# Fixed turns for PSUM places in an attention and expert kernel, and P V's bank emptied one operation earlier

## The chip, the cores and the metric

The kernel runs on one core of a Trainium2 chip. Its time is the device time of one execution in microseconds (us). An execution is profiled once for the trace; three plain runs give the median.

## The reference

Attention over 8 batches and 8 heads: queries are averaged in twos (1152 to 576 rows), keys and values have 1152 rows of 64. Its result feeds a mixture of 8 experts that sends each of 4608 rows to one expert.

```python
q_pool = q.reshape(B, H, S // factor, factor, D).mean(axis=3)
scores = scale * np.matmul(q_pool, k.transpose(0, 1, 3, 2))
scores = scores - np.max(scores, axis=-1, keepdims=True)
attn = np.exp(scores)
attn = attn / (np.sum(attn, axis=-1, keepdims=True) + 1e-09)
...
logits = x @ w_gate
e_idx = np.argmax(logits, axis=1)
...
    h = np.maximum(x[mask] @ w1[e], 0.0)
    ye = h @ w2[e]
    out[mask] = gate_w[mask, None] * eom[mask, e, None] * ye
```

## The kernel before, in words

Two stages follow each other: the attention with the router (`attention`, the first 1090 us), and the experts (`Moe.run`). The change is in the first alone.

The attention goes over 32 **pairs** of heads. A pair takes 18 **steps**: a step makes one **chunk** of 128 keys of one head (9 chunks a head). Four streams are interleaved step by step, and the instructions of TensorE, VectorE, ScalarE and GpSimd stand in exactly the order in which the Python code emits them (`manual_schedule`):

- **Scores** (`scores`, L269 to L296): four matmuls (L279, L281) into a PSUM place of two banks; ScalarE takes two exponentials of it. In most chunks they go to a float32 and a float16 tile (L293, L294), and GpSimd subtracts one from the other (L295). In chunks 1, 3, 7, 9, 13, 15 of a pair (and in all odd chunks of the last pair) the second exponential is written back into PSUM (L285, L286), and VectorE subtracts (`lo`, L289) in the next step; only then is the place free. There are two places.
- **Maxima** (`mgen`, L210 to L243): for a later pair the row maxima of the scores, matmuls L232 into a bank and a VectorE reduction L233. A step has one or two of them in turn, two in odd steps. Behind each, `pop()` emits one waiting small operation.
- **P V** (`av`, L298 to L328): per chunk 15 matmuls (L308 to L310) into the single bank `av`, in bursts of 1 to 3 chunks at the end of even steps. A head's P V ends in step 4 or 14 of a pair, and the next head's starts two steps later, in step 6 or 16. Between them three VectorE operations empty the bank: e0 (L317), e1 (reciprocal, L320), e2 (the division into `xb`, L323). They are put at the front of the list `fill`.
- **The router** (`logits`, `router`): transposes L370, logits L385, then some 20 tiny VectorE operations on a batch every fourth pair. It keeps a PSUM place over several steps, twice: `tl`, then `rk`, whose last reader is the sum `cum` (L473).

`fill` is the list of small operations; `pop` takes from its front. It is called at the start of each step, behind each maximum, and with everything at the start of a head's P V. So before the change e0 comes at the start of step 15, e1 behind its first maximum, e2 behind its second.

PSUM has 8 banks: two places of two banks for scores (pool `ps_s`), one bank for P V, three for maxima and all small matmuls (pool `ps_m`, tag `mp`). The pools have several buffers under one tag, and the building layer chooses the place when it lays out the program, so a place need not follow in turn. In the built program the 18 chunks of pair 10 use the score banks 2 0 2 2 0 2 0 2 0 2 0 2 0 2 0 0 2 0: chunks 3 and 15 take the place that the chunk before them has just used. Banks of `mp` are taken in turn, 903 of 1106 times the one used three allocations before; 27 times it is the one used last.

The experts' first weight split (ScalarE cast L733, VectorE subtraction L734) is not under the fixed order, so the layer places it among the attention's last steps.

Of the kernel before, what the change touches and what calls it, by code (L numbers as in the profile page):

```python
# [8 lines left out]
F32 = mybir.dt.float32  # L9
# [8 lines left out]
PSUM = bass.MemoryType.PSUM  # L18
# [41 lines left out]
def attention(tc, qT, kT, vL, wg, keep, xrows, idscr, cum, pairs, setup, scat, init):  # L60
    nc = tc.nc
    nb = len(pairs) // 4
    with ExitStack() as ctx:
        def pool(name, bufs=1, **kw):
            return ctx.enter_context(tc.tile_pool(name=name, bufs=bufs, **kw))
# [6 lines left out]
        ep = pool("a_e")  # L72
        lp = pool("a_l")
        p3 = pool("a_p3")
        ps_s = pool("ps_s", 2, space=PSUM)
        ps_a = pool("ps_a", 1, space=PSUM)
        ps_m = pool("ps_m", 3, space=PSUM)

        ident = keep['ident']
        onesf = keep['onesf']  # L80
# [22 lines left out]
        def prep(n, table):  # L103
# [67 lines left out]
                nc.scalar.activation(out=j, in_=vp[:, NC * h:NC * h + NC], func=AF.Abs, scale=2.0 ** -17, accum_out=am[:, h:h + 1])  # L171

            def gmax():
                g = ps_m.tile([128, 512], F32, name="tp", tag="mp")[:, 0:2]
                nc.tensor.matmul(g, lhsT=onesf, rhs=am, start=True, stop=True)
                gm.append(g)

# [21 lines left out]
            for r, name, *arg in table:  # L199
                f = P(fns[name], *arg)  # L200
# [9 lines left out]
        def mgen():  # L210

            for n in range(len(pairs)):
                st = states[n]
                ka, kb, qa, qb = st['ka'], st['kb'], st['qa'], st['qb']
                qbf = qb.rearrange("p h n -> p (h n)")
                for t0, t1 in ((0, 5), (5, 9)):
                    nt = t1 - t0
                    pm = sm.tile([128, 16], F32, name="pm")
                    ch = [(t, c) for t in range(t0, t1) for c in range(3)]
                    for i, (t, c) in enumerate(ch):  # L220
                        mp = ps_m.tile([128, 512], F32, name=f"mp{n}", tag="mp")[:, 0:384]
                        cs = slice(384 * c, 384 * c + 384)
                        ops = []
                        mt = mtile(t)
                        for (h, o) in mt:
                            ops.append((qa[:, o:o + 128], ka[:, h, cs]))
                            if len(mt) == 1:
                                ops.append((qb[0:66, h, 128 * t if h == 0 else 64 + 128 * (t - 5):][:, 0:128], kb[0:66, h, cs]))
                        if len(mt) == 2:
                            ops.append((st['qd'], st['kp'][:, cs]))  # L230
                        for j, (l, r) in enumerate(ops):
                            nc.tensor.matmul(mp, lhsT=l, rhs=r, start=j == 0, stop=j == len(ops) - 1)  # L232
                        nc.vector.tensor_reduce(out=pm[:, i:i + 1], in_=mp, axis=AX.X, op=ALU.max)  # L233
                        pop()
                        if i < len(ch) - 1:
                            yield
                    m9 = sm.tile([128, 5], F32, name="m9")

                    def ch0(m9=m9, pm=pm, nt=nt, t0=t0, t1=t1, qbf=qbf):
                        nc.vector.tensor_reduce(out=m9[:, 0:nt], in_=pm[:, 0:3 * nt].rearrange("p (t c) -> p t c", c=3), axis=AX.X, op=ALU.max)  # L240
                        pend_t.append((m9, nt, t0, t1, qbf, now[0]))
                    fill.append(ch0)
                    yield  # L243

        fill = []
        now = [0]

        def pop(k=1):
            while k and fill:
                fill.pop(0)()  # L250
                k -= 1
# [3 lines left out]
        def rows(force=False):  # L255
            while pend_t and (force or now[0] >= pend_t[0][-1] + TLAG):
                m9, nt, t0, t1, qbf, _ = pend_t.pop(0)
                tp = ps_m.tile([128, 512], F32, name="tp", tag="mp")[0:nt, 0:128]
                nc.tensor.transpose(out=tp, in_=m9[:, 0:nt], identity=ident)
                mr = sm.tile([5, 2, 128], F32R, name="mr")[0:nt]  # L260
                c0 = 16.0 * SHIFT
                nc.vector.tensor_scalar(out=mr[:, 0], in0=tp, scalar1=c0, scalar2=None, op0=ALU.subtract)
                nc.vector.scalar_tensor_tensor(out=mr[:, 1], in0=tp, scalar=c0, in1=mr.bitcast(F32)[:, 0], op0=ALU.subtract, op1=ALU.subtract)
                for j in range(2):
                    dmaf(qbf[66 + j:67 + j, 128 * t0:128 * t1].rearrange("o (t n) -> o t n", n=128), mr[:, j])
# [3 lines left out]
        def scores(st, h):  # L269
            ka, kb, qa, qb = st['ka'], st['kb'], st['qa'], st['qb']  # L270
            o = h * (NQ + 64)
            for c in range(NC):
# [1 line left out]
                ph = pp.tile([128, NQ], F16, name="ph", bufs=PB)  # L274
                pl = pp.tile([128, NQ], F16, name="pl", bufs=PB)
                st['ph', h, c], st['pl', h, c] = ph, pl
                sps = ps_s.tile([128, 2, 512], F32, name=f"sps{st['n']}", tag="sps")
                for j in range(2):
                    nc.tensor.matmul(sps[:, j, 0:288], lhsT=ka[:, h, ks], rhs=qa[:, o + 288 * j:o + 288 * j + 288], start=True, stop=False)  # L279
                for j in range(2):  # L280
# [1 line left out]
                x = sps[:, :, 0:288]  # L282
# [15 lines left out]
        def av(st, h, xb):  # L298
# [14 lines left out]
            r = sm.tile([128, 5], F32, name="r")  # L313
            H = 2 * st['p'][1] + h

            def e0():
                nc.vector.tensor_scalar(out=r, in0=av_[:, :, 64], scalar1=1e-9 * math.exp(SHIFT), scalar2=st['sc'][:, h:h + 1], op0=ALU.add, op1=ALU.mult)  # L317

            def e1():
                nc.vector.reciprocal(out=r, in_=r)  # L320

            def e2():
                nc.vector.tensor_tensor(out=xb[:, :, 64 * H:64 * H + 64], in0=av_[:, :, 0:64], in1=r.unsqueeze(2).broadcast_to([128, 5, 64]), op=ALU.mult)  # L323
                if h == 1:
                    routers.append([logits(st['p'][0], st['p'][1], xb), 0])
            fill[0:0] = [e0, e1, e2]
            pop(IMM)
            yield  # L328

        routers = []  # L330

        def psum():
            return ps_m.tile([128, 512], F32, name="tp", tag="mp")

        wf = bp.tile([128, 4, 16], F32, name="wf")
        wgt = bp.tile([128, 4, WC], F32R, name="wgt")
# [59 lines left out]
        def router(b, xb):  # L396
# [2 lines left out]
            tid = sm.tile([128, 5, IW], I32, name="tid", bufs=2)  # L399
            nc.gpsimd.iota(tid[:, 0:4], pattern=[[128, 4], [0, IW]], base=b * NQ, channel_multiplier=1)  # L400
            nc.gpsimd.iota(tid[:, 4], pattern=[[0, IW]], base=b * NQ + NQ - 128, channel_multiplier=1)
            tl = psum()

            def cut(x, o, *shape):
                n = math.prod(shape)
# [11 lines left out]
            g, og = lg[:, :, 0:8], lg[:, :, 8:16]  # L417
# [8 lines left out]
            e2 = sm.tile([128, 5, 8], F32, name="eq", bufs=2)  # L426
# [7 lines left out]
            V.tensor_tensor(out=ohb, in0=em8, in1=b8(em), op=ALU.is_equal)  # L434
            so = sm.tile([128, 5, 8], F32, name="so", bufs=2)
            V.tensor_tensor(out=so, in0=og, in1=ohb, op=ALU.mult)
            yield 1
            rk = psum()
            rv = cut(rk, 0, 5, 8)
            of = ohb.rearrange("p t e -> p (t e)")  # L440
            nc.tensor.matmul(rk[:, 0:40], lhsT=tri, rhs=of, start=True, stop=False)
# [29 lines left out]
            cs = cut(rk, 96, 8)  # L471
            V.tensor_reduce(out=cs, in_=ohb.rearrange("p t e -> p e t"), axis=AX.X, op=ALU.add)
            V.tensor_tensor(out=cum, in0=cs, in1=cum, op=ALU.add)  # L473
            for t in range(5):
                for _ in range(3):
                    yield
                i = nc.gpsimd.indirect_dma_start(
                    out=idscr, out_offset=bass.IndirectOffsetOnAxis(ap=pi[:, t:t + 1], axis=0),
                    in_=tid[:, t], in_offset=None, bounds_check=NID - 1, oob_is_err=False)
                for q in scat:  # L480
                    tc.declare_no_dep(i.ins, q, reason="distinct slots")
                scat.append(i.ins)
                if t == 2 and b < nb - 1:
                    wr()
# [19 lines left out]
        NP = len(pairs)  # L504
        pos = dict(m=0)
# [19 lines left out]
        with tc.manual_schedule(engines={E.PE, E.DVE, E.Activation, E.Pool}):  # L525
# [15 lines left out]
            for s in range(18 * NP + 14):  # L541
# [13 lines left out]
                prep_at(s, 1)  # L555
                adv('m', mg, mw)
                rows()
                j = s - ALAG
                for _ in range(BURST.get(j % 18, 0) if 0 <= j < 18 * NP else 0):
                    next(ag)  # L560
# [429 lines left out]
```

## Time and profile before

| | |
|---|---|
| plain runs | 1622.76, 1626.42, 1629.04 us; median 1626.42 |
| profiled execution | 1624.72 us, span 1622.7 us, mean granted clock 0.986 |
| TensorE busy | 1533.1 us (94%) |
| VectorE, ScalarE, GpSimd busy | 1073.4 (66%), 1078.5 (66%), 996.3 (61%) us |
| one pair in the steady attention | 32.1 us (360.8 to 392.9) |
| attention's last matmul of P V | 1080.4 us |

On the profile's timeline each row has the start (us from the span's start), the duration, the engine, the source line, the operation, output<-input and the shapes; in brackets stands how long the engine was idle before it and what ended that. PE is a matmul of TensorE, PEld a weight load, DVE VectorE, ACT ScalarE, POOL GpSimd, SP the queue that issues loads. A matmul starts before the one ahead of it has drained, so a bracket understates a loss on PE; the distance of two starts doesn't.

### The profile page before, as it was taken

The numbers are of one execution on the slowest core, as the hardware profiler recorded it, in microseconds if no ns is written. First come the engines' busy times: TensorE is split into PE (matmuls) and PEld (weight loads), VectorE is DVE, ScalarE is ACT, GpSimd is POOL, SyncE is SP. The second block draws the span as 40 slices with busy tenths as digits, with TensorE's granted clock in tenths as the row PEclk, the third lists the DMA queues.
The fourth block names the chain that finished last, engine by engine and source line by source line (L and its number), as shares of the span: only waits on it lengthen the run. The fifth ranks groups of instructions, "written<-read, shape, count | busy, mean of one in ns | idle before, by whom it ended". The sixth has DMA issues, their size and how long they took to land. (4 is left out here: it accounts for less than half of the span.)

```text
span 1622.7 us, 42199 instructions
## 1 busy us (share of the span) xinstructions
PE 1533.1 (94%) x16618; PEld 1411.1 (87%) x16618; DVE 1073.4 (66%) x2222; ACT 1078.5 (66%) x1862; POOL 996.3 (61%) x917
## 2 busy tenths in 40 slices
PE   4999999999999999999999999879999999999997
PEld 4898889888988888888888888868999999999996
DVE  4676776776676676676677767656666566656663
ACT  2887778877878787878777877744445444544541
POOL 4887888788879788879788978634222322232300
PEclk9999999999999999999999999979999999999999
DMA  7765455655566457446645664255454655263600
GB/s 207 217 160 143 133 149 149 156 139 141 152 151 158 124 144 189 129 123 175 158 129 153 161 154 127 83 173 196 168 190 156 213 176 194 94 226 107 208 22 25
DMA packets 88754, 245.48 MB, mean 151 GB/s; under 512 B 13082, under 2 KB 17370, under 8 KB 88546
## 3 DMA queue, kind: packets, MB, share of 16 engines
q1 hardware_dynamic: 78826, 221.07, 48.6%
q0 software_dynamic: 9728, 21.67, 4.2%
q8 instruction: 134, 2.20, 0.6%
q14 instruction: 66, 0.54, 0.1%
HBM read 165.04 MB, written 23.81 MB: 116 GB/s over the span
## 5 line engine op out<-in xcount | busy, mean ns | idle before, releaser
L233 DVE TENSOR_REDUCE pm<-mp 128x1 f32<-128x384 f32 x864 | 457.6, 549 | 263.3 <-PE mp L232 257.7
L295 POOL TENSOR_TENSOR pl<-p,ph 128x576 f16<-128x576 f32 x381 | 490.2, 1287 | 187.8 <-ACT ph L294 155.5
L232 PE MATMUL mp<-ka,qa 128*128 128x384 f32 x960 | 317.7, 347 | 20.2 <-DMA qa<-yq 18.5
L293 ACT ACTIVATE p<-sps 128x576 f32<-128x576 f32 x381 | 251.0, 659 | 116.8 <-PE sps L281 108.3
L308 PEld LDWEIGHTS <-ph 128*128 128x128 f16 x2880 | 262.6, 97 | 74.3 <-DVE xb L323 40.8
L308 PE MATMUL av<-vt,ph 128*128 128x65 f16 x2880 | 297.0, 194 | 23.4 <-DVE xb L323 23.4
L279 PE MATMUL sps<-qa,ka 128*128 128x288 f32 x1152 | 281.6, 326 | 16.7 <-ACT ph L294 10.9
L309 PE MATMUL av<-vt,ph 128*128 128x64 f16 x2880 | 294.7, 195 | 0.0
L310 PE MATMUL av<-vt,pl 128*128 128x65 f16 x2880 | 293.8, 193 | 0.0
L309 PEld LDWEIGHTS <-ph 128*128 128x128 f16 x2880 | 266.2, 97 | 0.4
L310 PEld LDWEIGHTS <-pl 128*128 128x128 f16 x2880 | 266.5, 99 | 0.0
L232 PE MATMUL mp<-kb,qb 66*128 66x384 f32 x768 | 262.5, 342 | 0.6 <-DMA kb<-kp 0.6
L281 PE MATMUL sps<-qb,kb 68*128 68x288 f32 x1152 | 248.5, 298 | 2.8 <-DMA qb<-mr 2.8
L294 ACT ACTIVATE ph<-sps 128x576 f16<-128x576 f32 x381 | 249.3, 654 | 0.0
L279 PEld LDWEIGHTS sps<-qa,ka 128*128 128x128 f32 x1152 | 183.5, 191 | 27.9 <-ACT ph L294 19.2
L764 PE MATMUL hps<-xh,w1h 128*128 128x256 f32 x704 | 200.4, 285 | 0.0
L764 PE MATMUL hps<-xl,w1h 128*128 128x256 f32 x704 | 200.3, 284 | 0.0
L232 PEld LDWEIGHTS mp<-ka,qa 128*128 128x128 f32 x960 | 180.4, 192 | 22.8 <-issue 18.5
L764 PE MATMUL hps<-xh,w1l 128*128 128x256 f32 x704 | 199.6, 284 | 0.0
L767 ACT ACTIVATE hh<-hps 128x512 fp32r<-128x512 f32 x88 | 52.7, 598 | 221.1 <-PE hps L764 221.1
L285 ACT ACTIVATE ph<-sps 128x576 f16<-128x576 f32 x195 | 128.9, 661 | 92.0 <-PE sps L281 89.7
L281 PEld LDWEIGHTS sps<-qb,kb 68*128 68x128 f32 x1152 | 186.7, 191 | 3.2 <-DMA qb<-mr 3.2
(170 smaller groups left out, 3184.6 us busy)
## 6 DMA issues: line engine op xcount, KB each, us to landing
ka<-xk SPq DMA_DIRECT2D x128, 288.0 KB
raw1b<-in_w_dram SPq DMA_DIRECT2D x24, 1024.0 KB
raw2b<-in_w_dram SPq DMA_DIRECT2D x24, 1024.0 KB
raw1a<-in_w_dram SPq DMA_DIRECT2D x22, 1024.0 KB
raw2a<-in_w_dram SPq DMA_DIRECT2D x22, 1024.0 KB
qp<-in_qT_dram SPq DMA_DIRECT2D x32, 576.0 KB
kpf<-in_kT_dram SPq DMA_DIRECT2D x32, 576.0 KB
vp<-in_vL_dram SPq DMA_DIRECT2D x32, 576.0 KB
```

The source lines that it names most:

```text
L232: nc.tensor.matmul(mp, lhsT=l, rhs=r, start=j == 0, stop=j == len(ops) - 1)
L233: nc.vector.tensor_reduce(out=pm[:, i:i + 1], in_=mp, axis=AX.X, op=ALU.max)
L279: nc.tensor.matmul(sps[:, j, 0:288], lhsT=ka[:, h, ks], rhs=qa[:, o + 288 * j:o + 288 * j + 288], start=True, stop=False)
L281: nc.tensor.matmul(sps[:, j, 0:288], lhsT=kb[:, h, ks], rhs=qb[:, h, 288 * j:288 * j + 288], start=False, stop=True)
L285: nc.scalar.activation(out=ph2, in_=x, func=AF.Exp, scale=1.0 / 16)
L293: nc.scalar.activation(out=p32.rearrange("p (j n) -> p j n", j=2), in_=x, func=AF.Exp, scale=1.0 / 16)
L294: nc.scalar.activation(out=ph2, in_=x, func=AF.Exp, scale=1.0 / 16)
L295: nc.gpsimd.tensor_tensor(out=pl, in0=p32, in1=ph, op=ALU.subtract)
L308: nc.tensor.matmul(av_[:, qb, 0:65], lhsT=hi, rhs=vt[:, h, c, 0:65], start=c == 0 and qb == 0, stop=False)
L309: nc.tensor.matmul(av_[:, qb, 0:64], lhsT=hi, rhs=vt[:, h, c, 66:130], start=False, stop=False)
L310: nc.tensor.matmul(av_[:, qb, 0:65], lhsT=lo, rhs=vt[:, h, c, 0:65], start=False, stop=c == NC - 1 and qb == 4)
L764: nc.tensor.matmul(hp[:, f], lhsT=W1[w][:, c, fs], rhs=d[x][:, c], start=i == 0, stop=i == 11)
```

## The change

It does three things.

1. **Places in fixed turn.** The score places get tags of their own, `sps0` and `sps1`, by the chunk's number: even chunks take one, odd ones the other. The three places of `ps_m` also get own tags, and a counter `ring` goes around them; a place that the router holds is skipped until it is given back (`ring[1].discard`).
2. **e0 and e1 are one entry of `fill`.** Both are emitted at the start of step 15 (or 5), e2 behind the step's first maximum, so ahead of its second.
3. **The last pair.** Once all maxima are done (`pos['m'] == 27 * NP`), each step emits two more small operations in their place.

```diff
-        ps_s = pool("ps_s", 2, space=PSUM)
+        ps_s = pool("ps_s", 1, space=PSUM)
         ps_a = pool("ps_a", 1, space=PSUM)
-        ps_m = pool("ps_m", 3, space=PSUM)
+        ps_m = pool("ps_m", 1, space=PSUM)
+        ring = [0, set()]
+
+        def psum(hold=False, name="tp"):
+
+            ring[0] = next(i % 3 for i in range(ring[0] + 1, ring[0] + 4) if i % 3 not in ring[1])
+            if hold:
+                ring[1].add(ring[0])
+            x = ps_m.tile([128, 512], F32, name=name, tag=f"mp{ring[0]}")
+            return (x, ring[0]) if hold else x
...
-                        mp = ps_m.tile([128, 512], F32, name=f"mp{n}", tag="mp")[:, 0:384]
+                        mp = psum(name=f"mp{n}")[:, 0:384]
...
-                sps = ps_s.tile([128, 2, 512], F32, name=f"sps{st['n']}", tag="sps")
+                sps = ps_s.tile([128, 2, 512], F32, name=f"sps{st['n']}", tag=f"sps{(c + 9 * h) % 2}")
...
-            def e0():
+            def e01():
                 nc.vector.tensor_scalar(out=r, in0=av_[:, :, 64], scalar1=1e-9 * math.exp(SHIFT), scalar2=st['sc'][:, h:h + 1], op0=ALU.add, op1=ALU.mult)
-
-            def e1():
                 nc.vector.reciprocal(out=r, in_=r)
...
-            fill[0:0] = [e0, e1, e2]
+            fill[0:0] = [e01, e2]
...
-            tl = psum()
+            tl, tk = psum(True)
...
+            ring[1].discard(tk)
             yield 1
-            rk = psum()
+            rk, rkk = psum(True)
...
             V.tensor_tensor(out=cum, in0=cs, in1=cum, op=ALU.add)
+            ring[1].discard(rkk)
...
                 rows()
+                if pos['m'] == 27 * NP:
+                    pop(2)
```

What moves in the order of instructions is little, nearly all of it on VectorE. First VectorE's queue at the end of a head's P V in pair 10, before the change: `av` is the bank, `mp` the maxima's banks, and `pl<-sps` is the subtraction L289.

```order
L233 TENSOR_REDUCE pm<-mp_7692 128x1
L317 TENSOR_SCALAR r<-av_7381,sc 128x5
L233 TENSOR_REDUCE pm<-mp_7723 128x1
L320 RECIPROCAL r<-r 128x5
L233 TENSOR_REDUCE pm<-mp_7729 128x1
L323 TENSOR_TENSOR xb<-av_7381,r 128x5x64
L289 TENSOR_TENSOR pl<-sps_7715,ph 128x576
```

The same place in VectorE's queue after the change (its line numbers are some 9 higher):

```order
L242 TENSOR_REDUCE pm<-mp_7692 128x1
L326 TENSOR_SCALAR r<-av_7381,sc 128x5
L327 RECIPROCAL r<-r 128x5
L242 TENSOR_REDUCE pm<-mp_7724 128x1
L330 TENSOR_TENSOR xb<-av_7381,r 128x5x64
L242 TENSOR_REDUCE pm<-mp_7730 128x1
L298 TENSOR_TENSOR pl<-sps_7716,ph 128x576
```

The reciprocal moved ahead of the step's first reduction, the division ahead of its second. Then VectorE's queue in the last pair, before the change; `w1l<-raw1a` is the experts' weight split.

```order
L317 TENSOR_SCALAR r<-av_21573,sc 128x5
L734 TENSOR_TENSOR w1l<-raw1a,w1h 128x1024
L289 TENSOR_TENSOR pl<-sps_21795,ph 128x576
L320 RECIPROCAL r<-r 128x5
L323 TENSOR_TENSOR xb<-av_21573,r 128x5x64
L734 TENSOR_TENSOR w1l<-raw1a,w1h 128x1024 x3
L289 TENSOR_TENSOR pl<-sps_21851,ph 128x576
```

And after it, the same place of VectorE's queue:

```order
L326 TENSOR_SCALAR r<-av_21573,sc 128x5
L327 RECIPROCAL r<-r 128x5
L330 TENSOR_TENSOR xb<-av_21573,r 128x5x64
L742 TENSOR_TENSOR w1l<-raw1a,w1h 128x1024
L298 TENSOR_TENSOR pl<-sps_21796,ph 128x576
L742 TENSOR_TENSOR w1l<-raw1a,w1h 128x1024
L298 TENSOR_TENSOR pl<-sps_21851,ph 128x576
```

All three operations that empty the bank now stand ahead of the weight split, whose four pieces are spread over more steps; ScalarE's casts L733 are spread in the same way. In the same pair one transpose of maxima (L259) now stands ahead of a burst of P V, and on the load queue one load of values stands ahead of a register load. GpSimd's order is the same.

More of the change, by code (lines that the diff above doesn't have):

```diff
@@ L173, in gmax @@
             def gmax():
-                g = ps_m.tile([128, 512], F32, name="tp", tag="mp")[:, 0:2]
+                g = psum()[:, 0:2]
                 nc.tensor.matmul(g, lhsT=onesf, rhs=am, start=True, stop=True)
@@ L257, in rows @@
                 m9, nt, t0, t1, qbf, _ = pend_t.pop(0)
-                tp = ps_m.tile([128, 512], F32, name="tp", tag="mp")[0:nt, 0:128]
+                tp = psum()[0:nt, 0:128]
                 nc.tensor.transpose(out=tp, in_=m9[:, 0:nt], identity=ident)
@@ L330, in attention @@
         routers = []
-        def psum():
-            return ps_m.tile([128, 512], F32, name="tp", tag="mp")
         wf = bp.tile([128, 4, 16], F32, name="wf")
```

## Prediction

> **What bounds the kernel now.** I read the page first, then stages of the span, then the list of waits, then single steps on the timeline. The profiled execution has a span of 1622.7 us and a time of 1624.72 us; the three plain runs have a median of 1626.42. A change of 0.5% (8.1 us) is about the least that a measurement of this kernel tells from none.
>
> The page's busy times, then two stages: the steady attention, and the last pair of heads with the router's tail. Columns of a stage: its length, busy time of PE, PEld, DVE, ACT, POOL, the granted clock, DMA share, GB/s.
>
> ```profile
> PE 1533.1 (94%) x16618; PEld 1411.1 (87%) x16618; DVE 1073.4 (66%) x2222; ACT 1078.5 (66%) x1862; POOL 996.3 (61%) x917
> ...
> 60.00:1043.00 983.00, 945.44 (x12521) 874.86 (x12520) 692.23 (x1730) 784.49 (x1462) 800.25 (x717) 1.00 0.57 145
> 1043.00:1091.00 48.00, 32.19 (x486) 28.97 (x484) 24.20 (x60) 28.98 (x53) 16.01 (x16) 0.82 0.50 186
> ```
>
> TensorE is the bound. In the attention it is idle for 983.00 - 945.44 = 37.6 us, in the last pair and the router's tail for 15.8. Nothing that the change touches lies in the expert stage behind them, so all of it is won or lost in these two stretches. What ends the idle time (total, number, longest):
>
> ```profile
> PE av L308 <- DVE xb L323: 23.4, 53, 3.5
> PE sps L279 <- ACT ph L294: 10.9, 25, 0.5
> PEld sps L279 <- ACT ph L294: 19.2, 54, 0.6
> ```
>
> P V's first matmul waits 53 times for the division that empties its bank (e2, L323); the scores wait some 54 times (25 long, the rest short) for ScalarE's second exponential. Matmuls overlap in the trace, so a gap understates a loss; I take losses from start to start.
>
> **Part 1: e2 ahead of the second maximum.** Step 15 to 17 of pair 10, where a head's P V ends:
>
> ```profile
> 386.83 0.73 DVE L289 TENSOR_TENSOR pl<-sps,ph 128x576 f16<-128x576 f32 x1
> ...
> 387.20 0.19 PE L308 MATMUL av<-vt,ph 128*128 128x65 f16 x1
> 387.21 0.65 ACT L294 ACTIVATE ph<-sps 128x576 f16<-128x576 f32 x1
> ...
> 387.91 0.53 PE L279 MATMUL sps<-qa,ka 128*128 128x288 f32 x2 [0.46 <-ACT ph L294]
> ...
> 389.09 0.56 DVE L233 TENSOR_REDUCE pm<-mp 128x1 f32<-128x384 f32 x1 [0.93 <-PE mp L232]
> 389.57 0.18 DVE L320 RECIPROCAL r<-r 128x5 f32<-128x5 f32 x1
> 389.66 0.52 DVE L233 TENSOR_REDUCE pm<-mp 128x1 f32<-128x384 f32 x1
> 389.95 0.33 PE L232 MATMUL mp<-kb,qb 66*128 66x384 f32 x1
> 390.10 0.48 DVE L323 TENSOR_TENSOR xb<-av,r 128x320 f32<-128x320 f32 x1
> 390.49 0.75 DVE L289 TENSOR_TENSOR pl<-sps,ph 128x576 f16<-128x576 f32 x1
> 390.63 0.20 PE L308 MATMUL av<-vt,ph 128*128 128x65 f16 x1 [0.35 <-DVE xb L323]
> ...
> 391.56 0.51 PE L279 MATMUL sps<-qa,ka 128*128 128x288 f32 x2
> ```
>
> And what a step looks like without these waits (pair 10, step 3), with a short wait of scores at its end:
>
> ```profile
> 364.74 0.34 PE L232 MATMUL mp<-kb,qb 66*128 66x384 f32 x1
> ...
> 364.92 0.20 PE L308 MATMUL av<-vt,ph 128*128 128x65 f16 x1
> ...
> 365.22 0.73 DVE L289 TENSOR_TENSOR pl<-sps,ph 128x576 f16<-128x576 f32 x1
> ...
> 365.75 0.19 PE L308 MATMUL av<-vt,ph 128*128 128x65 f16 x1
> ...
> 366.07 0.53 PE L279 MATMUL sps<-qa,ka 128*128 128x288 f32 x2
> ```
>
> Unhindered, P V starts 0.18 behind the maximum's matmul (364.74 to 364.92); here it starts 0.68 behind (389.95 to 390.63). Each such wait loses 0.50 us. After the change L320 stands ahead of the step's first maximum, in VectorE's idle 0.93, and L323 right behind that maximum: it starts at 389.57 (where L320 stood, which overlaps the end of the reduction), ends at 390.05, and P V may start 0.05 later (the delay from 387.86, where L294 ends, to 387.91): 390.10. TensorE is there at 390.13. The wait goes wholly, with 0.03 to spare. What comes behind: the second maximum is delayed by L323, but its place is wanted again only a step later, and the subtraction L289 moves forward, since L320 no longer stands ahead of it. The two long waits (3.5 and one of 2.3 below) are in the last pair; the other 51 give 51 x 0.50 = **25.5 us**. One VectorE rule speaks against it: the Trainium skill, "VectorE: DVE Perf Modes", section "The DRAIN you can't avoid", says that the next operation starts only when the pipe is empty; by that L323 would start some 0.08 later, and the term would be 51 x 0.05 = 2.6 less (my estimate). The rows disagree: L323 starts at 390.10 while the maximum before it runs to 390.18, and I keep 25.5.
>
> **Part 2: the scores' places in turn.** The waits for L294 arise because the place taken is that of the chunk just before. In strict turn a chunk takes the place of the chunk two before. For even chunks that one was freed by L294 long ago. For odd chunks it is freed by L289, the subtraction that reads PSUM, and this is a new wait.
>
> - Chunk 15 (387.91 above): the matmul before it starts at 387.20 and scores follow it 0.09 later where nothing waits, so 0.62 is lost. L289 of chunk 13 ends at 387.56; with 0.05 the new start is 387.61. Gain 0.30 here; in the pairs that hold the router's small operations VectorE is later, so I take 0.25: 25 x 0.25 = **6.3**.
> - Chunk 3 (366.07): lost 0.23 (365.75 + 0.09 = 365.84); L289 of chunk 1 ends at 365.95, new start 366.00. Gain 0.07, more in router pairs where the subtraction is early; I take 0.10 x 27 = **2.7**.
> - Chunk 17 (391.56): does not wait now. P V comes 0.50 earlier, so it would start at 391.06; L289 of chunk 15 now ends at 391.24, less some 0.08 since L320 is gone from in front of it, 391.16, plus 0.05. A new wait of 0.15 in most pairs, none where a wait of that size stands already: 26 x 0.10 = **-2.6**.
> - Chunk 9, behind the other head's end. ScalarE runs from 371.62 without a break, so its side does not move when TensorE does:
>
> ```profile
> 371.62 1.24 ACT L133 CAST xk<-kpf 128x576 fp32r<-128x576 f32 x2
> ...
> 372.37 0.20 PE L308 MATMUL av<-vt,ph 128*128 128x65 f16 x1 [0.35 <-DVE xb L323]
> ...
> 375.02 0.68 ACT L286 ACTIVATE sps<-sps 128x576 f32<-128x576 f32 x1
> ...
> 375.80 0.76 DVE L289 TENSOR_TENSOR pl<-sps,ph 128x576 f16<-128x576 f32 x1 [0.32 <-POOL pl L295]
> ...
> 376.81 0.38 PE L279 MATMUL sps<-qa,ka 128*128 128x288 f32 x1
> ```
>
> L289 of chunk 7 follows L286 (end 375.70) and ends at 376.56, so chunk 9 can start at 376.61. It started at 376.81 and now wants 376.31: 0.30 of the 0.50 is given back. Not in the seven router pairs, where part 3 holds TensorE back further: 19 x 0.30 = **-5.7**.
>
> **Part 3: the three places of maxima.** These mostly went in turn already. Where the router holds a place, the next transposes (L370) get, in the built program, exactly the place just given up:
>
> ```profile
> 341.84 0.33 PE L232 MATMUL mp<-kb,qb 66*128 66x384 f32 x1
> ...
> 342.47 0.44 PE L370 MATMUL tp<-ident,xb 128*128 128x128 f32 x2 [0.30 <-DVE pm L233]
> ...
> 343.06 0.17 DVE L473 TENSOR_TENSOR cum<-tp,cum 128x8 bf16<-128x8 f32 x1
> ```
>
> Unhindered they would start 0.18 behind that matmul, at 342.02; now they wait for a maximum's reduction and are 0.45 late. After the change they wait for the router's last reader, L473, which ends at 343.23: start 343.28, 0.81 later. Scores, maxima and P V are queued behind. Seven batches: 7 x 0.81 = **-5.7**. In the first pairs some maxima also take a later place; I allow **-1** (estimate). Bounds of parts 2 and 3 together: the waits go and none comes, at most 25 x 0.62 + 29 x 0.23 = +22; no gain on them and all new waits in full, 26 x (0.15 + 0.30) + 7 x 0.81 = -17. My sum is -6.0, between, because each term has its row.
>
> **Part 4: the last pair.** No maxima are left there, so before the change the small operations came one per step:
>
> ```profile
> 1051.19 0.43 PE L281 MATMUL sps<-qb,kb 68*128 68x288 f32 x2
> 1051.49 1.04 ACT L733 CAST w1h<-raw1a 128x1024 fp32r<-128x1024 f32 x1 [1.00 <-DMA raw1a<-in_w_dram]
> ...
> 1053.71 0.76 DVE L289 TENSOR_TENSOR pl<-sps,ph 128x576 f16<-128x576 f32 x1
> ...
> 1054.39 0.18 DVE L320 RECIPROCAL r<-r 128x5 f32<-128x5 f32 x1
> ...
> 1055.15 0.23 PE L308 MATMUL av<-vt,ph 128*128 128x65 f16 x1 [3.53 <-DVE xb L323]
> ...
> 1056.78 0.83 PE L279 MATMUL sps<-qa,ka 128*128 128x288 f32 x2
> ...
> 1073.09 0.20 PE L308 MATMUL av<-vt,ph 128*128 128x65 f16 x1 [2.29 <-DVE xb L323]
> ```
>
> L320 and L323 stood behind the experts' weight split (L734), which waits for the cast L733, which waits for a load. Now they come ahead of it, and both waits, 3.53 + 2.29 = 5.8, go. What is late next is chunk 7's place: L289 of chunk 5 ends at 1054.47, so those scores start at about 1054.5 and not at 1056.78, a gain of 2.2; the three other casts are now spread among the exponentials, which takes some back; at the second wait about 2 comes again, but the subtractions set the pace. I take **+3.5**, with 0 (all given back to ScalarE) and 5.8 as ends. The clock also falls there:
>
> ```profile
> 1054.00:1058.00 4.00, 2.85 (x35) 2.84 (x36) 3.37 (x5) 3.55 (x5) 1.29 (x1) 0.50 1.05 390
> ```
>
> The Trainium skill ("TensorE: Matmul & The Clock Gate", "Part 1: The HAM clock gate") says that about 3.4 us of idleness halve the clock; by that, with the 3.53 wait gone, the ten P V blocks behind it would take 0.93 as at 390.63, not 1.63, and the sum would be 0.7 higher (estimate). The row of clock 0.50 right after the wait agrees; I leave it out, as ScalarE sets the pace there.
>
> **Sum:** 25.5 + 6.3 + 2.7 - 2.6 - 5.7 - 5.7 - 1 + 3.5 = **23.0 us**. From 1624.72 that is 1601.7, from the median 1626.42 it is 1603.4. I say **1603**.
>
> **Rivals.**
> - *The waits move on* (0.13). Every 0.50 that P V gains is taken back at the next place, chunk 9 or chunk 17. Then 25.5 - 2.6 - 5.7 becomes 0 and 5.8 is left: 1620.6. For: ScalarE's unbroken stretch behind 371.62. Against: VectorE's idle 0.93 ahead of 389.09, and ScalarE at 784 of 983.
> - *Slower* (0.06): the subtraction becomes the bound. Four places per pair (chunks 3, 9, 15, 17) then hang on L289 with no slack, so if it comes x later than in these rows, 4 x 26 x x = 104x is lost; from x = 0.22 on the sum is negative. At x = 0.30, about half a reduction (0.56), it is 23.0 - 31.2: 1635. Against: at chunk 17 the order moves it forward.
> - *More* (0.10): earlier scores bring the exponentials and so L289 forward, and the new waits (2.6 + 5.7 + 5.7) do not come: 37 us, 1589.
> - That turn is not what frees the scores would cost only parts 2 and 3: 25.5 + 3.5 - 1 = 28, 1598, inside the forecast, which has 0.71 (1594 to 1613).
>
> **How the numbers follow.** The range reaches down to the middle of *more* and up to *the waits move on*: 1590 to 1619. Faster by over 0.5% means under 1618.3: 0.71 + 0.10 + 0.02 of the second case = 0.83; same 0.11; slower 0.06.
>
> **What would show it.** In the profile after: P V's wait for xb nearly gone; the scores' wait for L294 replaced by one for L289, 10 to 20 us in all; seven waits of about 1.3 at the transposes on the router's last operation; no wait over 2 us at P V in the last pair; the expert stage unchanged in length. I am wrong if P V's starts still wait, if scores wait for L289 at chunks 5 or 11 too, or if ScalarE's waits for scores vanish, which would make it the bound.

## The result and the profile after

| | before | after |
|---|---|---|
| plain runs | median 1626.42 us (1622.76 to 1629.49) | median 1612.38 us (1610.94 to 1615.64) |
| profiled execution | 1624.72 us, span 1622.7 | 1615.64 us, span 1613.5 |

The ratio is 0.9924, with a 95% interval of 0.9908 to 0.9939: 14.0 us faster by the medians (12.4 by the ratio), where 23.0 were predicted. The two profiled executions differ by 9.1 us only; a part of that difference is told below (pair 26).

In the changed kernel the line numbers are 9 higher here: the scores are L288 and L290, the exponentials L294/L295 and L302/L303, VectorE's subtraction L298, P V L317 to L319, e0, e1 and e2 L326, L327 and L330, the router's transposes L374 and its last operation L478. First the page's busy times, then three stages: the steady attention, the last pair with the router's tail, and the experts.

```profile
PE 1531.1 (95%) x16618; PEld 1415.6 (88%) x16618; DVE 1083.9 (67%) x2222; ACT 1077.8 (67%) x1862; POOL 997.9 (62%) x917
...
60.00:1031.00 971.00, 938.49 (x12457) 874.72 (x12454) 696.59 (x1718) 778.77 (x1454) 795.62 (x714) 1.00 0.58 147
1031.00:1081.00 50.00, 36.80 (x560) 33.07 (x559) 29.48 (x71) 34.59 (x62) 20.01 (x20) 0.89 0.47 174
1081.00:1613.00 532.00, 517.06 (x3337) 472.53 (x3337) 327.15 (x374) 238.57 (x301) 147.99 (x133) 0.98 0.46 153
```

TensorE's idle time in the attention fell from 37.6 to 971.00 - 938.49 = 32.5 us, that of the tail from 15.8 to 13.2; the experts take 532 us, as they did in the profile of before (1091 to 1623). The list of waits (total, number, longest) shows what took the place of the old ones:

```profile
PE sps L288 <- DVE pl L298: 17.8, 51, 1.6
...
PEld L317 <- DVE xb L330: 7.9, 50, 0.2
...
PE tp L374 <- DVE cum L478: 7.7, 7, 1.1
```

P V's wait for the division, 23.4 us before, is down to short waits of weight loads, none over 0.2. The scores now wait for VectorE's subtraction, 17.8 us, and the transposes for the router's last operation, seven times 1.1.

The end of a head in pair 10, the place that the prediction showed:

```profile
385.81 0.74 DVE L298 TENSOR_TENSOR pl<-sps,ph 128x576 f16<-128x576 f32 x1
...
386.24 0.19 PE L319 MATMUL av<-vt,pl 128*128 128x65 f16 x1
...
386.69 0.50 PE L288 MATMUL sps<-qa,ka 128*128 128x288 f32 x2 [0.26 <-DVE pl L298]
...
387.17 0.19 DVE L327 RECIPROCAL r<-r 128x5 f32<-128x5 f32 x1
...
388.32 0.48 DVE L330 TENSOR_TENSOR xb<-av,r 128x320 f32<-128x320 f32 x1
...
388.70 0.34 PE L241 MATMUL mp<-kb,qb 66*128 66x384 f32 x1
388.71 0.55 DVE L242 TENSOR_REDUCE pm<-mp 128x1 f32<-128x384 f32 x1
388.88 0.21 PE L317 MATMUL av<-vt,ph 128*128 128x65 f16 x1
...
389.18 0.75 DVE L298 TENSOR_TENSOR pl<-sps,ph 128x576 f16<-128x576 f32 x1
...
389.78 0.19 PE L319 MATMUL av<-vt,pl 128*128 128x65 f16 x1
...
390.07 0.50 PE L288 MATMUL sps<-qa,ka 128*128 128x288 f32 x2
```

P V starts 0.18 behind the maximum's matmul (388.70 to 388.88) where it started 0.68 behind: that loss is gone whole. But look at the two scores. Where nothing holds them, scores follow the last matmul of P V by 0.03, as chunk 17 does in the kernel before (0.028 ahead of rounding):

```profile
391.54 0.19 PE L310 MATMUL av<-vt,pl 128*128 128x65 f16 x1
391.56 0.51 PE L279 MATMUL sps<-qa,ka 128*128 128x288 f32 x2
```

(The prediction's 0.09 counts from the last L308, two matmuls further ahead.) After the change chunk 15 starts at 386.69, 0.45 behind the last matmul of P V, and its place was given back by the subtraction that ends at 385.81 + 0.74 = 386.55. Chunk 17 starts at 390.07, 0.29 behind, and the subtraction that gives its place back ended at 389.93. In both cases 0.14 lies between the end of the subtraction and the scores.

Chunk 9 in pair 11, with ScalarE's stretch ahead of it, shows the same, 406.37 + 0.76 = 407.13 to 407.28:

```profile
405.59 0.68 ACT L295 ACTIVATE sps<-sps 128x576 f32<-128x576 f32 x1
...
406.37 0.76 DVE L298 TENSOR_TENSOR pl<-sps,ph 128x576 f16<-128x576 f32 x1 [0.83 <-POOL pl L304]
...
407.28 0.50 PE L288 MATMUL sps<-qa,ka 128*128 128x288 f32 x2 [0.24 <-DVE pl L298]
```

The bracket of L298 names GpSimd, but the subtraction starts 0.10 behind the end of ScalarE's L295 (405.59 + 0.68 = 406.27), in this pair and in every other from 4 to 30, whenever GpSimd ends: it waits for the exponential.

The router's place in pair 9: the transposes wait for L478, as predicted, and start 1.44 behind the maximum's matmul:

```profile
339.50 0.34 PE L241 MATMUL mp<-kb,qb 66*128 66x384 f32 x1
...
340.72 0.17 DVE L478 TENSOR_TENSOR cum<-tp,cum 128x8 bf16<-128x8 f32 x1
340.94 0.44 PE L374 MATMUL tp<-ident,xb 128*128 128x128 f32 x2 [1.11 <-DVE cum L478]
```

And the last pair: e2 (L330) comes at once, and P V has no wait of 2 or 3.5 us any more. The scores wait for the subtraction instead, 1.56 at chunk 7, which starts at 1049.38, and 1.37 at chunk 13:

```profile
1045.90 0.49 DVE L330 TENSOR_TENSOR xb<-av,r 128x320 f32<-128x320 f32 x1
...
1048.57 0.76 DVE L298 TENSOR_TENSOR pl<-sps,ph 128x576 f16<-128x576 f32 x1
...
1049.38 0.53 PE L288 MATMUL sps<-qa,ka 128*128 128x288 f32 x2 [1.56 <-DVE pl L298]
...
1060.07 0.50 PE L288 MATMUL sps<-qa,ka 128*128 128x288 f32 x2 [1.37 <-DVE pl L298]
```

**Where the time went.** I sum losses from start to start. For P V and the transposes a loss is the distance from the matmul ahead of it beyond the lower quartile of the same two lines; for scores behind P V, the four chunks among them, it is the distance beyond 0.03. P V, all scores behind P V and the transposes are counted from 60 us to the start of the last pair, the four chunks over pairs 1 to 30.

| us lost at | before | division only | turns only | after | after, scores from a pool | after, router's place later |
|---|---|---|---|---|---|---|
| P V behind a maximum | 26.1 | 0 | 26.3 | 0 | 0 | 0 |
| all scores behind P V | 23.6 | 38.2 | 20.2 | 33.3 | 39.0 | 33.0 |
| of these chunk 3 | 5.8 | 5.8 | 5.5 | 5.4 | 5.9 | 5.5 |
| chunk 9 | 0.1 | 7.9 | 0.0 | 7.5 | 7.7 | 7.1 |
| chunk 15 | 16.1 | 15.2 | 13.1 | 13.1 | 16.2 | 13.1 |
| chunk 17 | 1.1 | 8.7 | 1.0 | 6.7 | 8.7 | 6.7 |
| router's transposes | 3.2 | 3.2 | 8.8 | 8.8 | 8.8 | 3.2 |

The middle columns are experiments of the next section. The column "after" against "before": 26.1 won at P V, 33.3 - 23.6 = 9.7 given back at the scores, 9.6 of it at the four chunks, 5.6 at the transposes. The last pair, from its first scores to the end of P V, takes 33.4 us instead of 37.5, a gain of 4.1.

One more piece stands in this profile and not in that of before, pair 26, where the kernel chooses the early expert with some tiny operations. The stretch from the scores' start in pair 26 to that in pair 27 takes 35.7 us, before it took 32.9:

```profile
888.84 2.68 POOL L145 TENSOR_TENSOR kp<-kpf,xk 128x1152 fp32r<-128x1152 f32 x1
...
890.75 3.38 DVE L656 TENSOR_TENSOR cn<-cn,mx 128x8 f32<-128x8 f32 x1
...
891.47 1.28 POOL L304 TENSOR_TENSOR pl<-p,ph 128x576 f16<-128x576 f32 x1
...
892.72 1.39 POOL L154 TENSOR_TENSOR yq<-yq,xq 128x576 fp32r<-128x576 f32 x1
...
894.65 0.39 PE L184 MATMUL tp<-am,onesf 128*128 128x2 f32 x2 [2.07 <-DVE pm L242]
```

The VectorE operation on 128x8 elements, 0.28 us in the profile of before, takes 3.38 here. It ends at 894.13, when GpSimd's third operation in a row ends (892.72 + 1.39 = 894.11), and VectorE's reductions and then TensorE wait behind it. In the profile of before the same operation began nearer to the end of the first of them (895.35 + 2.66 = 898.01) and ended 0.02 behind it:

```profile
895.35 2.66 POOL L136 TENSOR_TENSOR kp<-kpf,xk 128x1152 fp32r<-128x1152 f32 x1
...
897.75 0.28 DVE L648 TENSOR_TENSOR cn<-cn,mx 128x8 f32<-128x8 f32 x1
```

The profiles of experiments 2, 3 and 7 below have the same block, 3.19, 3.37 and 3.36 us long.

### The profile page after: what moved, and what is told of

Read it like the earlier page. It is cut to its first block, busy times and chain, and to the rows that moved or that the text cites. A ratio compares the mean times of both kernels' runs of the same rounds, so it can differ in the third digit from the quotient of the medians.

```text
span 1613.5 us, 42264 instructions
## 1 busy us (share of the span) xinstructions
PE 1531.1 (95%) x16618; PEld 1415.6 (88%) x16618; DVE 1083.9 (67%) x2222; ACT 1077.8 (67%) x1862; POOL 997.9 (62%) x917
## 5 line engine op out<-in xcount | busy, mean ns | idle before, releaser
L302 ACT ACTIVATE p<-sps 128x576 f32<-128x576 f32 x381 | 250.8, 658 | 115.3 <-PE sps L290 108.4
L288 PE MATMUL sps<-qa,ka 128*128 128x288 f32 x1152 | 280.3, 325 | 24.1 <-DVE pl L298 17.8
L317 PEld LDWEIGHTS <-ph 128*128 128x128 f16 x2880 | 261.8, 97 | 42.2 <-issue 29.5
L317 PE MATMUL av<-vt,ph 128*128 128x65 f16 x2880 | 295.7, 194 | 0.0
L319 PE MATMUL av<-vt,pl 128*128 128x65 f16 x2880 | 292.4, 192 | 0.0
L319 PEld LDWEIGHTS <-pl 128*128 128x128 f16 x2880 | 265.7, 99 | 0.0
L290 PE MATMUL sps<-qb,kb 68*128 68x288 f32 x1152 | 248.8, 298 | 2.0 <-DMA qb<-mr 2.0
L303 ACT ACTIVATE ph<-sps 128x576 f16<-128x576 f32 x381 | 249.4, 655 | 0.0
L288 PEld LDWEIGHTS sps<-qa,ka 128*128 128x128 f32 x1152 | 184.3, 192 | 36.6 <-PE av L319 22.3
L290 PEld LDWEIGHTS sps<-qb,kb 68*128 68x128 f32 x1152 | 187.4, 191 | 2.3 <-DMA qb<-mr 2.3
L294 ACT ACTIVATE ph<-sps 128x576 f16<-128x576 f32 x195 | 128.4, 658 | 84.2 <-PE sps L290 83.0
```

Of the source, the lines that this page charges most:

```text
L290: nc.tensor.matmul(sps[:, j, 0:288], lhsT=kb[:, h, ks], rhs=qb[:, h, 288 * j:288 * j + 288], start=False, stop=True)
L294: nc.scalar.activation(out=ph2, in_=x, func=AF.Exp, scale=1.0 / 16)
L302: nc.scalar.activation(out=p32.rearrange("p (j n) -> p j n", j=2), in_=x, func=AF.Exp, scale=1.0 / 16)
L303: nc.scalar.activation(out=ph2, in_=x, func=AF.Exp, scale=1.0 / 16)
L317: nc.tensor.matmul(av_[:, qb, 0:65], lhsT=hi, rhs=vt[:, h, c, 0:65], start=c == 0 and qb == 0, stop=False)
L319: nc.tensor.matmul(av_[:, qb, 0:65], lhsT=lo, rhs=vt[:, h, c, 0:65], start=False, stop=c == NC - 1 and qb == 4)
```

## The experiments

Eleven kernels, each against the kernel before: first each part of the change alone or left out, then three trials of what the new waits depend on, then two questions that these raised. The kernels of one group ran on the same chip, and the kernel before again with each group (medians 1624.0 to 1626.2 us), so across groups the ratios are what to compare.

**1. The division alone** (the kernel before, with this only):

```diff
-            def e0():
+            def e01():
...
-            def e1():
                 nc.vector.reciprocal(out=r, in_=r)
...
-            fill[0:0] = [e0, e1, e2]
+            fill[0:0] = [e01, e2]
```

> The kernel before with the second part of the change alone: e0 and e1 as one entry of the list, e2 behind the step's first maximum. Places and the last pair stay as before. Theory A (the terms add, with the sizes that the trace of the changed kernel shows): the 51 waits of P V of about 0.50 go (-25.5 us); the scores of chunk 9 wait 0.39 in 19 pairs (+7.4) and those of chunk 17 about 0.27 in 19 pairs (+5); chunks 3 and 15 still take the place used just before and lose as before. Sum about -13: near 1613 us, and P V shows no wait for xb in the steady pairs. Rival B (the parts only work together: with the places of before, the scores of chunk 15 and 17 give back what P V wins): 1620 us or more, with more waits of the scores for the second exponential than in the kernel before.

Median 1614.41 us (1611.72 to 1616.57), ratio 0.9929 (0.9909 to 0.995). This part alone gives as much as the whole change, as far as the intervals tell. The table's second column says how: 26.1 won, 14.6 given back at the scores (38.2 - 23.6), nearly all of it at chunk 9 (7.8) and 17 (7.6). Theory A holds, though chunk 17 gives back more than its 5. Rival B is right in kind (waits do move on) and wrong in size.

**2. The turns alone** (the kernel before with the tags of scores and maxima and the counter `ring`).

> The kernel before with the fixed turns alone, scores' places and maxima's places; e0, e1, e2 stand as before, one small operation per step in the last pair. Theory A: chunk 15 wins about 0.2 in 20 pairs (-4), chunk 3 nothing, the router's transposes lose 0.8 in seven batches (+5.6), P V waits as before: about +1 to +2 us, 1627 to 1628. Rival B (turns carry the gain): 1618 or less.

Median 1626.65 us, ratio 1.0002 (0.9988 to 1.0016): no difference. P V waits as before, and the gain of 3.4 at the scores is less than the 5.6 lost at the transposes. From this kernel's list of waits (P V for the division, scores for the subtraction):

```profile
PE av L317 <- DVE xb L332: 23.3, 53, 3.6
...
PE sps L288 <- DVE pl L298: 10.5, 31, 0.6
```

**3. Without the last pair's part:**

```diff
-                if pos['m'] == 27 * NP:
-                    pop(2)
```

> The changed kernel without the two extra small operations per step in the last pair. Theory A (the last pair is worth 3 to 4 us): near 1616 us, and the waits of 2 to 3.5 us of P V in the last pair are back. Rival B (ScalarE sets the pace of the last pair, what is won at P V is given back): 1612 to 1613, the last pair as long as in the changed kernel.

Median 1616.72 us, ratio 0.9937 (0.9917 to 0.9958). The interval overlaps that of the changed kernel, so the time alone does not decide; the trace does. The last pair takes 38.4 us here and 33.4 there, 5.0 us, and the long waits of P V are back. Its row in the list of waits, the longest at the end:

```profile
PEld L317 <- DVE xb L330: 14.0, 52, 3.8
```

**4. Scores' places from a pool of two again** (the rest of the change kept):

```diff
-        ps_s = pool("ps_s", 1, space=PSUM)
+        ps_s = pool("ps_s", 2, space=PSUM)
...
-                sps = ps_s.tile([128, 2, 512], F32, name=f"sps{st['n']}", tag=f"sps{(c + 9 * h) % 2}")
+                sps = ps_s.tile([128, 2, 512], F32, name=f"sps{st['n']}", tag="sps")
```

> The changed kernel with the scores' places from a pool of two again, so that chunks 3 and 15 of each pair take the place used just before. Theory A (the scores' turn is worth little, as the subtraction comes late): chunk 15 loses 0.62 again where it loses 0.42 in turn, chunk 3 about as much either way: 1614 to 1617 us. Rival B (my prediction's size for the turn, 6.3 + 2.7): 1620 to 1621. Rival C (the turn harms): under 1612.

Median 1617.17 us (1616.37 to 1620.67), ratio 0.9948 (0.9929 to 0.9968), just above the upper edge of A; the interval overlaps that of the changed kernel. In the trace the turn of the scores is worth 39.0 - 33.3 = 5.7 us: 3.1 at chunk 15, 2.0 at chunk 17, 0.5 at chunk 3, 0.2 at chunk 9.

**5. The subtraction of chunk 7 given to GpSimd, that of chunk 5 to VectorE:**

```diff
-PLP = (1, 3, 7, 9, 13, 15)
+PLP = (1, 3, 5, 9, 13, 15)
```

> The changed kernel, but VectorE subtracts chunk 5 instead of chunk 7 (GpSimd takes chunk 7). Theory A (the scores of chunk 9 wait 0.4 in some 20 pairs because their place is given back by VectorE's subtraction of chunk 7, 0.86 behind ScalarE's exponential): the wait at chunk 9 goes, nothing new at chunk 7, where the place is free 1.1 early: 8 us less, about 1605 us. Rival B (ScalarE's unbroken stretch around chunks 6 to 8 is the limit): the wait turns up at chunks 10 to 12 or at P V as a wait for an exponential: 1611 to 1613 us.

Median 1619.33 us (1614.40 to 1622.49), ratio 0.9964 (0.9953 to 0.9976): slower than the changed kernel, and neither forecast. The wait at chunk 9 did go, from 7.5 us to 0.0, so the cause is the one that theory A names and not ScalarE's stretch. But chunk 7 got a new wait, 0.27 in ordinary pairs and 0.83 in the router's, 11.2 us in all. I had reckoned with 1.1 us to spare at chunk 7 and forgotten that the subtraction of chunk 5 comes 1.2 behind ScalarE's end: in step 6 it stands in VectorE's queue behind e2 and a reduction.

**6. Subtractions moved away from all four places:**

```diff
-PLP = (1, 3, 7, 9, 13, 15)
+PLP = (2, 3, 5, 9, 11, 12)
```

> The changed kernel with VectorE's subtractions in chunks 2, 3, 5, 9, 11, 12 instead of 1, 3, 7, 9, 13, 15. Theory A (in turn, the four waits at chunks 3, 9, 15 and 17 all come from the subtraction that gives the place back late; per pair 0.26 + 0.40 + 0.42 + 0.27 us): all four go, chunks 4, 5, 7, 13, 14 have 0.7 to 1.5 us to spare: 25 to 30 us less, 1582 to 1588 us. Rival B (VectorE has no room in the other steps, or GpSimd and ScalarE take the pace once the scores run free): half or less of it, 1598 to 1612 us, and new waits at P V or at the maxima.

Median 1604.99 us (1602.36 to 1608.15), ratio 0.988 (0.9859 to 0.9902). All four waits went to 0.0, as theory A said, yet a good part of the gain is missing, as B said. Two places hold some of it: chunk 7's new wait of experiment 5 is here too (11.2 us), and pair 26 takes 39.3 us, since its VectorE operation is blocked for 7.39 us, past five GpSimd operations on the timeline:

```profile
876.24 2.68 POOL L145 TENSOR_TENSOR kp<-kpf,xk 128x1152 fp32r<-128x1152 f32 x1
...
876.58 7.39 DVE L656 TENSOR_TENSOR cn<-cn,mx 128x8 f32<-128x8 f32 x1
...
878.85 2.52 POOL L304 TENSOR_TENSOR pl<-p,ph 128x576 f16<-128x576 f32 x2
...
881.32 1.40 POOL L154 TENSOR_TENSOR yq<-yq,xq 128x576 fp32r<-128x576 f32 x1
...
882.67 1.27 POOL L304 TENSOR_TENSOR pl<-p,ph 128x576 f16<-128x576 f32 x1
```

**7. The router's place given back at the end of the step** (the changed kernel otherwise):

```diff
-            ring[1].discard(rkk)
+            late.append(rkk)
...
                         r[1] = next(r[0], 0)
+                while late:
+                    ring[1].discard(late.pop())
```

> The changed kernel, but the router's second PSUM place is given back at the end of the step, so that the next pair's transposes take the place of an older maximum. Theory A (the transposes wait for the router's last operation because the turn gives them just this place): the seven waits of about 1.1 to 1.4 go, 0.8 each: 5 to 6 us less, about 1607 us. Rival B (the scores behind them wait for the subtraction anyway): 1611 to 1613 us.

Median 1609.94 us over six executions, 1608.32 without a single one of 2090.67, which is left out of the ratio: 0.9907 (0.9888 to 0.9926). The interval overlaps that of the changed kernel, so the time alone does not decide. The trace is clear: the transposes lose 3.2 us instead of 8.8, as in the kernel before, and 16 steady pairs (8 to 24) take 510.7 us instead of 514.8, 1.0 for each router batch in them. Theory A.

**8. The early expert's counts in PSUM:**

```diff
-        cp = psum()
+        cp, ck = psum(True)
...
-        cn = kp.tile([128, 8], F32, name="cn1")
+        cn = cp[:, 8:16]
...
         V.tensor_reduce(out=mx, in_=cn, axis=AX.X, op=ALU.min)
+        psum.give(ck)
```

> The changed kernel with the eight counts of the early expert's choice kept in PSUM instead of SBUF, so that VectorE's comparison of them reads one SBUF tensor and not two. Theory A (the comparison that took 3.38 us in the profiled run stands behind GpSimd's work because both want SBUF, and it does so in some executions and not in others): it takes about 0.2 to 0.3 us in the profile, the plain runs lie within 1.5 us of each other near the lower times seen, 1611 us. Rival B (the 3.38 us come from something else, such as a late start of the instruction): the operation is as long again, and the times still fall in two groups 4 us apart.

Median 1614.64 us (1610.77 to 1616.80), ratio 0.9932 (0.9915 to 0.9948). The operation took 0.17 us beside the same GpSimd work, and pair 26 took 32.9 us, so the block's cause is shown: both inputs lay in SBUF.

```profile
891.82 2.66 POOL L146 TENSOR_TENSOR kp<-kpf,xk 128x1152 fp32r<-128x1152 f32 x1
...
893.75 0.17 DVE L657 TENSOR_TENSOR tp<-tp,mx 128x8 f32<-128x8 f32 x1
```

But the spread of the times stayed, and this half of theory A falls: the block is not what sets the executions apart, or not alone. Two things took time instead in this profile. The place that is now held makes one more batch of transposes wait (9.9 us lost there against 8.8). And the start was longer: pairs 0 and 1 took 68.1 us, with the clock at half for 13.7 us from 36.3 us on, against 64.9 us and 10.2 us in the changed kernel's.

**9. Subtractions in chunks 0, 2, 3, 9, 11, 12:**

> The changed kernel with VectorE's subtractions in chunks 0, 2, 3, 9, 11, 12. In the run with 2, 3, 5, 9, 11, 12 the waits at chunks 3, 9, 15 and 17 were gone and one at chunk 7 was new (0.27 in ordinary pairs, 0.82 in the router's), because the subtraction of chunk 5 comes 1.2 behind ScalarE: it stands behind the division e2 and a reduction. Theory A: without chunk 5 that wait goes too, 20 x 0.27 + 7 x 0.82 = 11 us, and nothing takes its place, since chunk 2 has 1.18 to spare and the subtraction of an even chunk takes 0.79: about 1594 us, 1590 to 1597. Rival B (VectorE or ScalarE take the pace once the scores run free): 1600 to 1606 us, with the wait at another chunk.

Median 1604.34 us (1599.85 to 1612.28), ratio 0.987 (0.9845 to 0.9896). Chunk 7's wait is gone and a new one is there, at chunk 8 in one pair of each four (the one in which the router's rows are written out), and it is not the engines that B names. ScalarE stands idle for 2.11 us ahead of the cast of the keys, and the scores wait for the exponentials behind it (start of the row, duration; SPq is SP's queue, which issues loads):

```profile
364.90 1.24 POOL L203 TENSOR_TENSOR vt<-vp,vt 128x576 f16<-128x576 f32 x1
...
366.18 0.33 SPq L138 DMA_DIRECT2D vp<-in_vL_dram  x1
...
366.56 0.63 SPq L135 DMA_DIRECT2D kpf<-in_kT_dram  x1
...
371.53 1.25 ACT L142 CAST xk<-kpf 128x576 fp32r<-128x576 f32 x2 [2.11 <-issue]
...
373.92 0.57 PE L288 MATMUL sps<-qa,ka 128*128 128x288 f32 x1 [1.74 <-ACT ph L303]
```

The profile names no releaser ("issue"), but the order of the rows does: the load of the values waits until GpSimd has read their buffer (366.14), the load of the keys stands behind it in SP's queue, and the cast follows 5 us after its issue. The keys' load is issued 7.8 us into the pair (366.56, the pair starts at 358.74), in the changed kernel 5.4.

**10. Experiments 7, 8 and 9 together.**

> The same, and the router's place given back at the end of the step (worth 0.25 per pair in its run, 7 to 8 us in the attention), and the counts of the early expert in PSUM (its operation was 3.38 us behind GpSimd in the changed kernel's profile and 7.39 us with the subtractions moved). Theory A (the three add): 1594 less 6 to 8 less 3 to 7: about 1584 us, 1578 to 1588. Rival B (they share waits): 1588 to 1594 us.

Median 1601.18 us (1597.16 to 1605.29), ratio 0.9851 (0.9829 to 0.9872). The forecast failed with that of 9: the wait at chunk 8 costs 10.2 us in four router pairs here (8.8 in experiment 9), and what the transposes won does not show in the length of pairs 8 to 24 (510.2 us, 509.4 in experiment 9).

**11. The same, keys' load first:**

```diff
-        (53, 'lv'), (71, 'amax', 0), (74, 'amax', 1), (81, 'gmax'), (82, 'scale', 0), (85, 'scale', 1), (90, 'scale', 2), (93, 'vh', 0), (93, 'vs', 0), (96, 'vh', 1), (97, 'vl', 0), (100, 'vs', 1), (104, 'vl', 1))
+        (55, 'lv'), (71, 'amax', 0), (74, 'amax', 1), (81, 'gmax'), (82, 'scale', 0), (85, 'scale', 1), (90, 'scale', 2), (93, 'vh', 0), (93, 'vs', 0), (96, 'vh', 1), (97, 'vl', 0), (100, 'vs', 1), (104, 'vl', 1))
```

> The last kernel with one number of the preparation's table changed, so that in the router's pairs the load of the values stands behind the load of the keys in SP's queue and not ahead of it. In the two runs before, ScalarE stood idle 2 to 4 us in each router pair ahead of the cast of the keys, 8.8 and 10.2 us of TensorE's loss in four pairs, and the keys' load had been issued only when the values' buffer came free (366.18, the GpSimd operation that reads it ended at 366.15). Theory A (the late load is what holds ScalarE and behind it the scores of chunk 8): these waits go, six pairs of 2 to 2.5 us: 12 to 15 us less, 1586 to 1590 us. Rival B (the keys' load comes late because the memory is busy, or GpSimd is the limit there): 1598 to 1602 us, with the same idle time of ScalarE.

Median 1589.06 us (1586.16 to 1594.75), ratio 0.9774 (0.9757 to 0.9791). Theory A, and the fastest version: 37 us below the kernel before by the ratio (0.0226 x 1624.43), 23 below the changed one by the medians. On the timeline, in the same pair, the load of the keys is issued 12.6 us ahead of its cast, where it was 5.0, and ScalarE does not wait for it. Further on, another of the early expert's operations is now blocked by GpSimd, for 2.69 us:

```profile
351.26 1.38 SPq L137 DMA_DIRECT2D kpf<-in_kT_dram  x1
...
363.84 1.25 ACT L144 CAST xk<-kpf 128x576 fp32r<-128x576 f32 x2
...
877.00 1.43 POOL L156 TENSOR_TENSOR yq<-yq,xq 128x576 fp32r<-128x576 f32 x1
877.01 2.69 DVE L667 TENSOR_TENSOR oh<-em,mx 128x8 f32<-128x8 f32 x1
```

The same stretch of the span, 290 to 815 us, in the changed kernel and then in this one (columns as before; TensorE is busy for 508.05 and for 517.01 of 525 us):

```profile
290.00:815.00 525.00, 508.05 (x6773) 473.33 (x6772) 375.94 (x927) 423.85 (x790) 434.22 (x389) 1.00 0.59 149
```

```profile
290.00:815.00 525.00, 517.01 (x6951) 483.11 (x6950) 384.07 (x949) 430.76 (x815) 442.06 (x397) 1.00 0.61 152
```

## Why the prediction was right, and where its sizes were off

The direction, the mechanism and the range (1590 to 1619) held; the size was 14.0 of 23.0, and the range held with one part 10 us off because it was 29 us wide. By its own steps, in us won (against the table above, and the profiled executions):

| step | predicted | measured |
|---|---|---|
| P V's starts | 25.5 | 26.1 |
| chunk 3 | 2.7 | 0.4 |
| chunk 9 | -5.7 | -7.4 |
| chunk 15 | 6.3 | 3.0 |
| chunk 17 | -2.6 | -5.6 |
| router's transposes | -5.7 | -5.6 |
| first pairs | -1 | 0 (pair 2 starts at 99.24 in both) |
| last pair | 3.5 | 4.1 |

- **P V.** Right: the reciprocal ahead of the first maximum and the division behind it end early enough, and experiment 1 shows that this part alone carries the gain. The 2.6 us that the rule of the Trainium skill ("VectorE: DVE Perf Modes", "The DRAIN you can't avoid") would have cost are not seen: no P V start is late, and the reduction behind L330 starts at 388.71, 0.09 ahead of the recorded end of L330 (388.32 + 0.48).
- **The scores' turn** is the step that was mis-sized: I had 6.3 + 2.7 - 2.6 - 5.7 = +0.7, and it is 0.4 - 7.4 + 3.0 - 5.6 = -9.6. The four waits came where they were forecast, behind L298, but each lasts longer. The prediction put 0.05 between the end of the operation that frees a place and the scores, read where ScalarE's L294 frees it (387.86 to 387.91). Behind VectorE's subtraction it is 0.14 to 0.15 in the rows of chunks 15, 17 and 9 above, and the median of the waiting cases is 0.146 at each of the four chunks. They wait in 27 (chunk 3), 18 (chunk 9), 27 (chunk 15) and 30 (chunk 17) cases, 102 in all: 102 x 0.096 = 9.8 us, nearly the whole of the 10.3 missing. It fits chunk by chunk too: 2.6, 1.7, 2.6 and 2.9 us of hand-over against 2.3, 1.7, 3.3 and 3.0 missing. The largest rest is at chunk 15: in ordinary pairs it won 0.20 (0.30 forecast), but in the seven router pairs it loses 0.67 where it lost 0.55 (medians).
- **The router's place.** Right to 0.1 us, and experiment 7 takes it back.
- **The last pair.** Right in size (4.1; experiment 3, the change without this part, is 5.0 longer there), and right in what is late next: L298 paces it. Chunk 7's place was put down as the next wait, and it waits 1.56.
- **What the sum did not hold.** The terms as measured give 26.1 - 9.6 - 5.6 + 4.1 = 15.0 us. The profiled execution won 9.1. Of the 5.9 between them 2.8 lie in pair 26 (35.7, and 32.9 in experiment 8, where the block is gone), 1.0 at scores behind transposes in two pairs, 1.5 between the matmuls of the maxima (8.2 beyond the lower quartile, 6.7 before), of which 0.4 lie in pair 26 and so are counted twice; about 1 is not placed. The plain runs, whose median won 14.0, have no trace. That not all of them hold the block of pair 26 would fit, but isn't shown, and experiment 8, without the block, spreads as widely (1610.77 to 1616.80) about a median no lower.
- **The rivals.** *The waits move on* is true of a part: 13.0 of the 26.1 came back at chunks 9 and 17, not all of it. *Slower* has the right mechanism, four places per pair without slack behind the subtraction, and it is 0.1 late, not the 0.22 from which it decides. *More* is out: none of the new waits stayed away. That the turn is not what frees the scores is out by experiment 4: chunks 15 and 17 lose 3.1 and 2.0 us more from a pool, and chunk 3 0.5.

Is the subtraction the limit that is left? Experiment 5 says yes for chunk 9, experiments 6 and 9 for all four: with the subtraction moved to other chunks these waits vanish. They also say that no chunk is free of charge: chunk 5 pays through e2, and the moved work of GpSimd pays through a buffer, a queue and a load.

## What to carry to other kernels

When a wait is removed, work out which event frees the next resource in line and by how much it precedes the need, for each place in the period, with the hand-over time read from a row of that very pair of operations; here 0.1 us, wrong in 102 places, was two fifths of the forecast gain. A fixed turn of buffers pays only where the one that frees the older buffer is early: moving the freeing operation (the subtraction) was worth more here than the turn, once it was moved to the right chunks. And an idle engine for which the profile names no releaser may wait for a load that is itself queued behind another load, so the issue times in the loads' queue are read too.

## What the runs showed of the hardware

- A VectorE operation of 128x8 elements with both inputs in SBUF took 3.38 us in the changed kernel, 7.39 in experiment 6 and 2.69 (another such operation) in experiment 11, each time until a GpSimd operation had ended; with one input in PSUM it took 0.17 (experiment 8). The Trainium skill, "SBUF — State Buffer", section "Who interferes with whom", says that a VectorE instruction with two SBUF inputs contends with a GpSimd instruction that reads SBUF, and calls the shared port pair an exclusive lock. The traces agree, and show more: VectorE did not always get its turn at the end of the GpSimd operation under way, but after three (3.38) and five (7.39) of them. In the kernel before and in experiments 1, 4, 5 and 9 the same operation began 0.26 to 0.31 ahead of the end of the same GpSimd operation, and got its turn there (0.28 to 0.33 us); where it began 0.56 or more ahead of it (the changed kernel, experiments 2, 3, 6 and 7), it was passed over. What decides this was not tried.
- From the end of an operation that frees a PSUM place to the matmul that takes it: 0.05 us behind ScalarE's exponential, 0.146 behind VectorE's subtraction; P V followed VectorE's division (L323, 390.10 + 0.48) by 0.05 in the profile of before, and by 0.058 in the median of its waits there. What makes the difference between the two VectorE operations no run here shows.
- In the first 60 us the granted clock is at half for 3.4 us (experiment 1) to 17.1 us (experiment 3), and pairs 0 and 1 take 64.4 us (experiment 1) to 68.1 us (experiment 8), though not in step with it. This may be a part of the spread between executions; it was not tried.
